# Strip 1's first product at two Strassen levels, with the further sums of W_in made by GpSimd in strip 0's second product and five of seven blocks used where they are made

## Chip, cores and metric

One core of one Trainium2 chip. The metric is the device time of one launch in microseconds (us). The engines are named PE (matrix products), DVE (VectorE), ACT (ScalarE), POOL (GpSimd) and SP, which here issues nearly all DMAs.

## The reference

```
kv  = einsum('bhsd,bhse->bhde', k, v)          # q, k, v: 8 x 8 x 576 x 64, f32
o   = einsum('bhsd,bhde->bhse', q, kv)
x   = o / sqrt(mean(o*o, -1) + 1e-6) * g_norm  # -> x: 4608 tokens x 512
h   = x @ w_in                                 # 512 x 2048
out = max(h, 0)**2 @ w_out                     # 2048 x 512
```

The attention part is small; the two products of the feed-forward part (x @ W_in, "first product", and g @ W_out, "second product", with g the squared relu) are nearly all of PE's work. w_in and w_out come as 64-bit floats, which the kernel turns into f32 itself.

## The kernel before

**Tiles and strips.** The 4608 tokens are nine strips of 512 (four tiles of 128). For each strip s the kernel does the first product, then the second. Meanwhile the queries of later strips are worked into x: a list of slices (`attend`, transposes, query products, means, roots, scaling, transposes of x), some after every step.

**Strassen.** The products are done with seven block products in place of eight (Winograd's form), on one or on two levels. Block sums of the weights are made once, those of x and g for each strip.

- Strip 0: first product plain (`up_first`); second product one level (`down`), in the order p = 1, 2, 5, 6, 7, 3, 4, two steps each: 14 steps, of which "step m" below is the m-th from 0. A block is 32 matmuls 128x256.
- Strip 1: first product one level (`up`: 4 groups g by 7 products p, 28 steps of 8 matmuls 128x256); second product two levels (`down_deep`).
- Strips 2 to 8: both on two levels: `up_slot` with 55 slots, in which 49 small products (`up_small`, 16 half-width matmul instructions each) run, then `down_deep`.

**The sums of the weights.** First-level sums of W_in: `sums_in(g)`, for each of four groups one scaling by g_norm on ACT (line 316) and four operations 128x512 on DVE (lines 318 and 306), at the steps 7, 8, 9 and 12 of strip 0's second product. The second-level ("deep") sums of W_out: `store_deep_sums(p, w)` after each block p of that product (4 operations 128x512 on DVE, `w_t` at line 306), stored to `w_deep` in DRAM by a DMA; strips 1 to 8 stream them back as `w_blk`. For p = 6 and p = 4 the four w_t are separate tiles of the `sum` pool with a store each (line 1000), for the others one tile of the `stream` pool with one store (line 1006). The second-level sums of W_in: `deep_sums_in(b)` for blocks b = 0 to 6, three POOL operations 128x512 each (lines 1219 and 306, tile `w_i`), made during strip 1's first product, stored to `w_in_deep` and streamed back by strips 2 to 8.

**What sets the order.** The order on each engine is the order in which the code writes it; nothing reorders. SP issues the DMAs in that same order, on one queue, with eight semaphores in turn, so a DMA is not issued before the eighth before it has landed. A pool hands out its tiles in turn: a new tile waits until all readers of its former contents, DMAs included, are done. `stream_pool` has 6 tiles of 1 MB, `sum_pool` 8 tiles of 256 KB, both opened where strip 0's second product starts. SP's queue around the change, in order: the stores of W_out's sums (`w_out<-wt`, `store_first` at line 344: 512 KB each), two loads `w_blk<-w_out` of 1 MB, two stores `w_deep<-w_t`, two of `store_first(2)`, a third `w_blk`, an output, k, v, k, v, a fourth `w_blk`, a `w_deep` store, the four stores of p = 6's w_t, the rest loads of k and v, queries.

**Names.** On PE the matmuls of a one-level product are line 870, those of two-level products line 865, the query products line 484 (`x_ps`), key-value products line 448 (`kv_ps`); ACT copies kv_ps to `kv_all` at lines 453 and 454, and query products read kv_all. Before block p = 3 of strip 0's second product, DVE makes `gq[21] - gq[11]` (line 306, 128x2048, `gt<-gt`; written at line 1034), which this block reads. `o_sb` at line 1042 is DVE's sum of a finished PSUM bank with a copy (`snap`) of another; it frees the bank for a later product. In strip 1's `up` the relu-square is DVE's lines 933 and 934.

Of the kernel before, what the change touches and what calls it, by code (L numbers as in the profile page):

```python
# [10 lines left out]
FP32 = mybir.dt.float32  # L11
# [9 lines left out]
def kernel(  # L21
# [52 lines left out]
    DEEP_UP = 2  # L74
# [3 lines left out]
    BEHIND = 1.6  # L78
    X_ON_PE = 2
# [234 lines left out]
    def sums_in(g):  # L314

        nc.scalar.activation(w_in[:, :, g, 0:4], w_in[:, :, g, 0:4], AF.Copy, scale=g_col)
        a11, a21, a12, a22, s1, s2, s4 = (block(b)[:, :, g] for b in range(7))
        nc.vector.tensor_tensor(out=s1, in0=a21, in1=a22, op=ALU.add)
        minus(nc.vector, s2, s1, a11)
        minus(nc.vector, s4, a12, s2)  # L320
        minus(nc.vector, a21, a11, a21)
# [366 lines left out]
    xc = {}  # L688

    def halves(s, kh, th):  # L690
        return xt[s][:, ts(th, TH // SQ), ts(kh, KH), :]

    def sums_x(s):
        xc[s] = t1, t2, t3, t4 = [
            sum_pool.tile([P, TH // SQ, KH, SQ], FP32, name=f"x_t{i}", tag="sum") for i in range(4)
        ]
        x = lambda kh, th: halves(s, kh, th)
        minus(nc.vector, t1, x(0, 1), x(0, 0))
        minus(nc.vector, t2, x(1, 1), t1)
        minus(nc.vector, t3, x(1, 1), x(0, 1))  # L700
        minus(nc.vector, t4, x(1, 0), t2)
# [218 lines left out]
    def up(s, g, p):  # L920
        open_bank(p)
        rhs = {
            1: halves(s, 0, 0), 2: halves(s, 1, 0), 3: halves(s, 1, 1),
            4: xc[s][3], 5: xc[s][0], 6: xc[s][1], 7: xc[s][2],
        }[p]
        for i in range(2):
            product(p, i, lambda kc: block(A_IN[p])[:, kc, g, ts(i, P)], lambda kc: rhs[:, :, kc, :], KH)
        dest = quarters(s, g)

        def relu_squared(q):  # L930
            def f(b, a):
                o = dest[q]
                nc.vector.tensor_tensor(out=o, in0=b, in1=a, op=ALU.add)
                nc.vector.scalar_tensor_tensor(out=o, in0=o, scalar=0.0, in1=o, op0=ALU.max, op1=ALU.mult)
            return f

        def last(b):
            nc.scalar.activation(dest[21], b, AF.Relu)
            nc.scalar.activation(dest[21], dest[21], AF.Square)

        combine(p, relu_squared(11), relu_squared(12), last, relu_squared(22))

# [3 lines left out]
    UP_SETS = (1, 6, 7, 5, 2, 3, 4)  # L946
    to_stream = [(s, p) for s in range(DEEP) for p in ORDER if (s, p) not in w_blk]
    for s in range(DEEP, N_STRIP):
        to_stream += [("in", s, p) for p in UP_SETS if s >= DEEP_UP]
        to_stream += [(s, p, n) for p in DEEP_ORDER for n in range(2)]  # L950
# [41 lines left out]
    def store_deep_sums(p, w):  # L992
        if p in (6, 4):

            parts = [sum_pool.tile([P, FQ // 2, P], FP32, name=f"w_t{i}", tag="sum") for i in range(4)]
            for _ in deep_sums(parts, w):
                if p == 4:
                    yield
            for i, t in enumerate(parts):
                nc.sync.dma_start(out=w_deep[B_OUT[p], :, i], in_=t)  # L1000
            return
# [3 lines left out]
        deque(deep_sums([t[:, i] for i in range(4)], w), 0)  # L1005
# [204 lines left out]

    def deep_sums_in(b):

        if b == 0:
# [289 lines left out]
```

## Time and profile before

| | |
|---|---|
| time, 3 runs | 868.7 us median (867.19 to 870.31) |
| profiled execution | 868.8 us, span of its instructions 867.0 us |
| granted TensorE clock | 1.000 |
| PE | 857.8 us busy, 99% |
| DVE | 702.0 us, 81% |
| ACT, POOL | 348.9 us (40%), 328.1 us (38%) |
| DMA | 236.46 MB, mean 273 GB/s |
| strip 0's second product | 83.1 to 138.25 us |
| strip 1's first product | 138.25 to 195.13 us |

How to read the rows of the prediction: a row of the timeline gives start, length (us), engine, line, operation, output tile <- input tiles, sizes and count, and in brackets the idle time before it with what ended it. A row of a table by stretches gives its limits and length, then the busy time of PE, PE's weight loads, DVE, ACT and POOL (number of instructions in brackets), the granted clock, the share of time in which the DMA engines were busy, and GB/s. A row of 40 digits gives the busy tenths of 40 equal slices of the span.

### The profile page before, as it was taken

Reading aid. Unit: us, or ns where it says so; the run is one execution under the profiler, and the core shown is the slowest. Engines: PE = TensorE matmul, PEld = TensorE weight load, DVE = VectorE, ACT = ScalarE, POOL = GpSimd, SP = SyncE. Lnnn points to the kernel's source line nnn. Section 1 sums busy time; section 2 is a strip of 40 time slices with the busy share of each in tenths; the row PEclk is TensorE's granted clock in tenths of the full one; section 3 lists DMA queues with packets and bytes.
Section 4 is the critical chain, followed back from the end, with each engine's and each line's share of the span. In section 5 each row is a group of like instructions: output and inputs, shape, how many; then the busy total and the mean of one; then the engine's idle time right before and its main releaser. Section 6 shows DMA issues by size and latency. Waiting matters only on the chain.

```text
span 867.0 us, 32426 instructions
## 1 busy us (share of the span) xinstructions
PE 857.8 (99%) x14176; PEld 804.2 (93%) x14176; DVE 702.0 (81%) x1132; ACT 348.9 (40%) x777; POOL 328.1 (38%) x335
## 2 busy tenths in 40 slices
PE   7999999999999999999999999999999999999998
PEld 6445888889999999999999999999999999999998
DVE  3768988879877996789688967897889777975887
ACT  4888241320048303750356034901491148102810
POOL 1223004630458223730574045704470447145700
PEclk9999999999999999999999999999999999999999
DMA  9898998999999997989698979987678856885583
GB/s 307 277 362 269 274 377 239 295 332 353 280 264 259 342 325 233 228 307 344 209 244 273 341 239 281 283 297 270 198 236 302 301 165 221 293 282 196 175 315 121
DMA packets 169469, 236.46 MB, mean 273 GB/s; under 512 B 78704, under 2 KB 133744, under 8 KB 161008
## 3 DMA queue, kind: packets, MB, share of 16 engines
q1 hardware_dynamic: 169024, 234.33, 83.5%
q8 instruction: 111, 1.82, 0.9%
q14 instruction: 30, 0.25, 0.1%
q10 hardware_dynamic: 304, 0.07, 0.0%
HBM read 197.66 MB, written 36.70 MB: 270 GB/s over the span
## 4 chain that ended last, share of the span: by engine, by line
PE 83%; DMA 7%; DVE 5%; ACT 3%; SPq 1%; issue 1%; DVEq 0%; ACTq 0%
PE ps_A L865 36%; PE ps_B L865 31%; PE ps_C L865 5%; PE ps_A L870 4%; DMA raw<-in_moe_w_in_dram 2%; PE kv_ps L448 2%; PE x_ps L484 2%; PE ps_B L870 2%; DVE w_t L306 1%; DMA w_deep<-w_t 1%; DMA raw<-in_moe_w_out_dram 1%; DMA w_blk<-w_deep 1%; PE ps_C L870 1%; DMA first_qkv<-in_v_dram 1%; ACT w_c L260 1%
## 5 line engine op out<-in xcount | busy, mean ns | idle before, releaser
L865 PE MATMUL ps_B<-w_blk,g_s 128*64 128x128 f32 x2016 | 122.0, 273 | 0.0
L865 PEld LDWEIGHTS ps_B<-w_blk,g_s 128*64 128x64 f32 x2016 | 112.6, 137 | 0.1
L306 POOL TENSOR_TENSOR x_l<-xT 128x256 f32<-128x256 f32 x21 | 16.2, 773 | 230.2 <-PE ps_A L865 230.2
L865 PE MATMUL ps_B<-w_blk,gt 128*64 128x128 f32 x1504 | 94.1, 273 | 0.3 <-DMA w_blk<-w_deep 0.3
L865 PE MATMUL ps_A<-w_blk,g_s 128*64 128x128 f32 x1536 | 92.2, 273 | 0.0
L1323 POOL TENSOR_TENSOR snap<-snap,gt 128x512 f32<-128x512 f32 x35 | 46.2, 1320 | 112.5 <-ACT snap L1328 93.6
L865 PEld LDWEIGHTS ps_A<-w_blk,g_s 128*64 128x64 f32 x1536 | 85.7, 137 | 0.0
L865 PEld LDWEIGHTS ps_B<-w_blk,gt 128*64 128x64 f32 x1504 | 84.6, 137 | 0.8 <-PE ps_B L865 0.5
L1328 ACT COPY snap<-ps_A 128x512 f32<-128x512 f32 x63 | 36.8, 585 | 103.6 <-PE ps_A L865 96.2
L1263 ACT ACTIVATE gt<-gt 128x512 f32<-128x512 f32 x112 | 70.2, 627 | 9.9 <-DVE gt L1323 9.9
L1264 ACT ACTIVATE gt<-gt 128x512 f32<-128x512 f32 x112 | 70.7, 631 | 3.5
L865 PE MATMUL ps_A<-w_blk,gt 128*64 128x128 f32 x1152 | 71.2, 273 | 0.0
L865 PEld LDWEIGHTS ps_A<-w_blk,gt 128*64 128x64 f32 x1152 | 64.7, 137 | 0.0
L1112 ACT COPY o_sb<-ps_A 128x128 f32<-128x128 f32 x24 | 6.4, 265 | 144.7 <-PE ps_A L865 109.4
L306 DVE TENSOR_TENSOR gt<-gt 128x2048 f32<-128x2048 f32 (+1 forms) x29 | 59.7, 2063 | 0.0
L1111 DVE TENSOR_TENSOR o_sb<-o_sb,ps_B 128x256 f32<-128x256 f32 (+1 forms) x123 | 47.4, 386 | 14.3 <-ACT o_sb L1112 9.5
L865 PE MATMUL ps_A<-x_l,w_in 128*64 128x128 f32 x896 | 58.6, 273 | 0.2 <-DVE gt L1323 0.2
L1323 POOL TENSOR_TENSOR gt<-gt,snap 128x512 f32<-128x512 f32 x42 | 52.5, 1279 | 15.1 <-DVE snap L1323 15.1
L865 PEld LDWEIGHTS ps_A<-x_l,w_in 128*64 128x64 f32 x896 | 50.8, 137 | 0.5 <-DVE gt L1323 0.5
L865 PE MATMUL ps_B<-x_l,w_blk 128*64 128x128 f32 x784 | 51.2, 273 | 0.0
L865 PE MATMUL ps_A<-x_l,w_blk 128*64 128x128 f32 x784 | 51.2, 273 | 0.0
L1112 ACT COPY o_sb<-ps_B 128x128 f32<-128x128 f32 x31 | 8.2, 265 | 96.3 <-PE ps_B L865 96.3
(214 smaller groups left out, 1900.2 us busy)
## 6 DMA issues: line engine op xcount, KB each, us to landing
w_blk<-w_deep SPq DMA_DIRECT2D x56, 1024.0 KB, 7.3
w_blk<-w_out SPq DMA_DIRECT2D x56, 768.0 KB, 6.2
w_blk<-w_in_deep SPq DMA_DIRECT2D x49, 768.0 KB, 5.8
raw<-in_moe_w_in_dram SPq DMA_DIRECT2D x16, 512.0 KB, 9.2
raw<-in_moe_w_out_dram SPq DMA_DIRECT2D x16, 512.0 KB, 8.0
k<-in_k_dram SPq DMA_DIRECT2D x29, 256.0 KB, 4.9
v<-in_v_dram SPq DMA_DIRECT2D x29, 256.0 KB, 5.2
x_d<-x_q SPq DMA_DIRECT2D x27, 256.0 KB, 4.8
```

Of the source, the lines that this page charges most:

```text
L260: nc.scalar.activation(c, high_f, AF.Copy, scale=EXPONENT)
L306: eng.tensor_tensor(out=out, in0=a, in1=b, op=ALU.subtract)
L448: nc.tensor.matmul(ps[ts(h, D), i], lhsT=a, rhs=w, start=i == 0 and c == 0, stop=c == C, skip_group_check=True)
L484: nc.tensor.matmul(ps[half, r, i, ts(p, D)], lhsT=q[row, half], rhs=kvd[b, p][row, row], start=True, stop=True)
L865: nc.tensor.matmul(ps[half], lhsT=lhsT[:, half], rhs=rhs, start=start, stop=stop, skip_group_check=True)
L870: nc.tensor.matmul(bank[BANK[p]][:, i, :], lhsT=lhsT(k), rhs=rhs(k), start=p in (1, 5, 2) and i == 0 and k == 0, stop=k == n - 1, skip_gro ...
L1111: add = lambda out, a, b: nc.vector.tensor_tensor(out=out, in0=a, in1=b, op=ALU.add)
L1112: yield nc.scalar.copy(q[:, 3:4], small(1))
L1263: nc.scalar.activation(o, o, AF.Relu)
L1264: nc.scalar.activation(o, o, AF.Square)
L1323: add = lambda eng, out, a, b: eng.tensor_tensor(out=out, in0=a, in1=b, op=ALU.add)
L1328: nc.scalar.copy(t, ps)
```

## The change

- Strip 1's first product becomes `up_slot`, on two levels; `up` and `sums_x` go. The sums of x for it (`leaf_x`, `sum_x`) are made by POOL, queued at step 8 of strip 0's second product.
- The scaling of W_in on ACT moves from steps 7, 8, 9, 12 to steps 0 and 1 (two instructions each); DVE's four operations of a pair of groups become 128x1024 and stand at steps 7 to 10, two a step.
- `deep_sums_in` moves into strip 0's second product: block 2 at step 1, block 3 at step 3, block 0 at 5, block 5 at 9, block 1 at 10; blocks 4 and 6 at the slots 2 and 24 of strip 1. Blocks 0, 2 and 3 are made in three tiles each of the `sum` pool and stored by three 256 KB DMAs, the others in a `stream` tile. The stores are queued on SP at the steps 3, 5, 7, 11 and 13 and at slots 8 and 31. Strip 1 reads blocks 0, 1, 4, 5 and 6 where they were made and streams 2 and 3 back.
- The w_t of p = 4, the last block, stay in SBUF for strip 1's second product (two loads fewer); they are made at the slots 38 to 43.
- `store_first` leaves out a quarter that nothing reads (256 KB of 1 MB, three times).
- In strip 1, the `snap` of j = 6 is DVE's sum instead of an ACT copy and a POOL sum. The pace of `attend` is halved per step, as there are twice as many.

The diff, cut to its core:

```diff
-    DEEP_UP = 2
+    DEEP_UP = 1
+    LATER = 2
...
+    SUMS_IN = {1: 2, 3: 3, 5: 0, 9: 5, 10: 1}
...
-    def sums_in(g):
-        nc.scalar.activation(w_in[:, :, g, 0:4], w_in[:, :, g, 0:4], AF.Copy, scale=g_col)
-        a11, a21, a12, a22, s1, s2, s4 = (block(b)[:, :, g] for b in range(7))
-        nc.vector.tensor_tensor(out=s1, in0=a21, in1=a22, op=ALU.add)
-        minus(nc.vector, s2, s1, a11)
-        minus(nc.vector, s4, a12, s2)
-        minus(nc.vector, a21, a11, a21)
+    def scales_in(h):
+        for g in range(2 * h, 2 * h + 2):
+            nc.scalar.activation(w_in[:, :, g, 0:4], w_in[:, :, g, 0:4], AF.Copy, scale=g_col)
+    def sums_in(h, n):
+        gs = slice(2 * h, 2 * h + 2)
+        a11, a21, a12, a22, s1, s2, s4 = (block(b)[:, :, gs] for b in range(7))
+        if n == 0:
+            nc.vector.tensor_tensor(out=s1, in0=a21, in1=a22, op=ALU.add)
+            minus(nc.vector, s2, s1, a11)
+        else:
+            minus(nc.vector, s4, a12, s2)
+            minus(nc.vector, a21, a11, a21)
...
     def store_first(b):
-        for e in range(2):
-            nc.sync.dma_start(out=w_out[b, :, e], in_=w_first[b][:, :, ts(e, P)])
+        for e, fs in enumerate((slice(FQ // 2, FQ), slice(0, FQ))):
+            nc.sync.dma_start(out=w_out[b, :, e, fs], in_=w_first[b][:, fs, ts(e, P)])
...
-    def up(s, g, p):
...
+    STORED_IN = (2, 3)
+        to_stream += [("in", s, p) for p in UP_SETS if s >= LATER or A_IN[p] in STORED_IN]
+        to_stream += [(s, p, n) for p in DEEP_ORDER for n in range(2) if s > DEEP or p != DEEP_ORDER[0]]
...
-                w_blk[u] = t.rearrange("p n f e -> p n (f e)")
-                nc.sync.dma_start(out=w_blk[u][:, 0:3], in_=w_in_deep[A_IN[p]].rearrange("p n g e -> p n (g e)"))
+                w = t.rearrange("p n f e -> p n (f e)")
+                nc.sync.dma_start(out=w[:, 0:3], in_=w_in_deep[A_IN[p]].rearrange("p n g e -> p n (g e)"))
+                w_blk[u] = [w[:, n] for n in range(3)]
...
     def store_deep_sums(p, w):
-        if p in (6, 4):
+        if p == 6:
...
-            for _ in deep_sums(parts, w):
-                if p == 4:
-                    yield
+            deque(deep_sums(parts, w), 0)
...
                 nc.sync.dma_start(out=w_deep[B_OUT[p], :, i], in_=t)
...
         t = deep.pop(p)
-        deque(deep_sums([t[:, i] for i in range(4)], w), 0)
+        if p == DEEP_ORDER[0]:
+            for j, x in zip((5, 6, 7, 4), range(4)):
+                w_blk[DEEP, p, j] = t[:, x]
+            for j, x in zip((3, 1, 2), ((0, 1), (1, 0), (1, 1))):
+                w_blk[DEEP, p, j] = w[:, x[0], ts(x[1], FQ // 2)]
+        for _ in deep_sums([t[:, i] for i in range(4)], w):
+            if p == DEEP_ORDER[0]:
+                yield
         nc.sync.dma_start(out=w_deep[B_OUT[p]], in_=t)
...
+    in_due = deque()
     def deep_sums_in(b):
...
-        if b == 0:
+        if b in (0, *STORED_IN):
...
+            t = [x.rearrange("p f e -> p (f e)") for x in t]
+            in_due.extend((w_in_deep[b, :, n].rearrange("p g e -> p (g e)"), x) for n, x in enumerate(t))
...
+            whole = whole[:, 0:3].rearrange("p n f e -> p n (f e)")
...
-        s1, s2, s4 = (x.rearrange("p f e -> p (f e)").rearrange("p (g e) -> p g e", g=2) for x in t)
+            in_due.append((w_in_deep[b].rearrange("p n g e -> p n (g e)"), whole))
+        s1, s2, s4 = (x.rearrange("p (g e) -> p g e", g=2) for x in t)
         nc.gpsimd.tensor_tensor(out=s1, in0=w_half(b, 0, 1), in1=w_half(b, 1, 1), op=ALU.add)
         minus(nc.gpsimd, s2, s1, w_half(b, 0, 0))
         minus(nc.gpsimd, s4, w_half(b, 1, 0), s2)
-        if b == 0:
-            for n, x in enumerate((s1, s2, s4)):
-                nc.sync.dma_start(out=w_in_deep[b, :, n], in_=x)
-            return
-        nc.sync.dma_start(
-            out=w_in_deep[b].rearrange("p n g e -> p n (g e)"), in_=whole[:, 0:3].rearrange("p n f e -> p n (f e)")
-        )
+        if b not in STORED_IN:
+            w_blk["in", DEEP_UP, next(p for p in UP_SETS if A_IN[p] == b)] = t
+    def store_sums_in():
+        while in_due:
+            to, x = in_due.popleft()
+            nc.sync.dma_start(out=to, in_=x)
...
         minus(nc.gpsimd, w_half(b, 0, 1), w_half(b, 0, 0), w_half(b, 0, 1))
...
+    MADE_IN, last_sums = {2: 4, 24: 6}, []
...
-        if slot in (1, 3, 5):
+        if slot in (1, 3, 5) and s > DEEP_UP:
...
-        if slot == 5:
+        if slot == 5 and s > DEEP_UP:
...
+        if s == DEEP_UP:
+            if slot in MADE_IN:
+                deep_sums_in(MADE_IN[slot])
+            if slot in (8, 31):
+                store_sums_in()
+            if slot == 38:
+                last_sums.append(store_deep_sums(*deep_due.popleft()))
+            if slot in (38, 39, 41, 43):
+                next(last_sums[0], None)
...
-                w = w_blk["in", s, p][:, (5, 6, 3).index(j), ts(i, P)]
+                w = w_blk["in", s, p][(5, 6, 3).index(j)][:, ts(i, P)]
...
-        if j == 3:
+        if j == 3 and (s > DEEP_UP or n in (1, 3, 5, 6)):
...
-            if j == 6 or before is None or p == 5:
+            if j == 6 and s > DEEP_UP or before is None or p == 5:
...
-        elif s == 0:
+        else:
...
-        else:
-            steps = [(1, up, (s, g, p)) for g in range(NG) for p in ORDER]
...
-        if s >= DEEP_UP:
-            goal = max(goal, min(ready[DEEP_UP] + (len(slices) - ready[DEEP_UP]) * (s - 1) // (N_STRIP - DEEP_UP - 1), len(slices)))
-            if s > DEEP_UP:
+        if s >= LATER:
+            goal = max(goal, min(ready[LATER] + (len(slices) - ready[LATER]) * (s - 1) // (N_STRIP - LATER - 1), len(slices)))
+            if s > LATER:
...
-                clock[0] += 3.2 if i >= n_up else 2.2 if s == DEEP else 1.2
+                clock[0] += 3.2 if i >= n_up else 1.1 if s == DEEP else 1.2
...
-                    attend(begun + (goal - begun) * min(i + 1, 25) // 25)
+                    attend(begun + (goal - begun) * min(i + 1, 50) // 50)
...
-                    attend_between(i, begun, goal, *(2, 34) if s == DEEP_UP else (0, 27), 38)
-                if s == DEEP and i in (3, 4, 7, 9):
-                    if i == 3:
-                        last_sums = store_deep_sums(*deep_due.popleft())
-                    next(last_sums, None)
-                if s == DEEP and i == n_up - 3:
-                    leaf_sums(s, 4)
-                if s == 1 and i in range(2, 23, 3):
-                    deep_sums_in((1, 6, 5, 4, 0, 2, 3)[i // 3])
-                if s == 1 and i in (17, 20, 21, 23):
-                    stream()
+                    attend_between(i, begun, goal, *(2, 34) if s == LATER else (0, 27), 38)
...
-            if i - n_up in (7, 8, 9, 12):
-                sums_in((7, 8, 9, 12).index(i - n_up))
-            if i == n_up + 11:
-                sums_x(1)
+            m = i - n_up
+            if m in (0, 1):
+                scales_in(m)
+            if 7 <= m < 11:
+                sums_in(*divmod(m - 7, 2))
...
-            pairs, m = divmod(max(n - 2 * NP, 0), 3)
-            attend(min(ready[0] + min(max(n, 0), 2 * NP) + (n >= 2 * NP) + 4 * pairs + (0, 2, 2)[m], goal))
+            pairs, third = divmod(max(n - 2 * NP, 0), 3)
+            attend(min(ready[0] + min(max(n, 0), 2 * NP) + (n >= 2 * NP) + 4 * pairs + (0, 2, 2)[third], goal))
             while deep_due and i not in (n_up + 1, n_up + 4, n_up + 12, n_up + 13):
                 deque(store_deep_sums(*deep_due.popleft()), 0)
+            if m in (3, 5, 7, 11, 13):
+                store_sums_in()
+            if m in SUMS_IN:
+                deep_sums_in(SUMS_IN[m])
+            if m == 8:
+                leaf_x(1, 0)
+                sum_x(1, 5)
+                sum_x(1, 6)
+                leaf_x(1, 1)
...
                 store_first(2)
```

More of the change, by code (lines that the diff above doesn't have):

```diff
@@ L686, in fetch_x @@
             )
-    xc = {}
     def halves(s, kh, th):
         return xt[s][:, ts(th, TH // SQ), ts(kh, KH), :]
[L693 to L701, printed above, removed]
     slices, ready = [], {}
@@ L918, in up_first @@
             nc.scalar.activation(dest[(11, 12, 21, 22)[2 * fh + th]][:, i, :], ps[:, ts(th, TH)], AF.Square)
-    def up(s, g, p):
[L921 to L941, printed above, removed]
     for p, t in zip((1, 2, 5), w_first):
@@ L946 @@
     UP_SETS = (1, 6, 7, 5, 2, 3, 4)
+    STORED_IN = (2, 3)
     to_stream = [(s, p) for s in range(DEEP) for p in ORDER if (s, p) not in w_blk]
     for s in range(DEEP, N_STRIP):
-        to_stream += [("in", s, p) for p in UP_SETS if s >= DEEP_UP]
-        to_stream += [(s, p, n) for p in DEEP_ORDER for n in range(2)]
+        to_stream += [("in", s, p) for p in UP_SETS if s >= LATER or A_IN[p] in STORED_IN]
+        to_stream += [(s, p, n) for p in DEEP_ORDER for n in range(2) if s > DEEP or p != DEEP_ORDER[0]]
     to_stream = iter(to_stream)
@@ L1360 @@
         attend(ready[s])
-        if s == DEEP_UP - 1:
+        if s == LATER - 1:
             while queried:
```

## The prediction

> **What bounds the kernel now.** I read the page's engine totals and chain, then the table by stages, then the single rows of the stages that the change touches.
>
> ```profile
> span 867.0 us, 32426 instructions
> PE   7999999999999999999999999999999999999998
> PE 83%; DMA 7%; DVE 5%; ACT 3%; SPq 1%; issue 1%; DVEq 0%; ACTq 0%
> ```
>
> PE is 99% busy (857.8 of 867.0 us): work taken off PE is time won, and a stall of PE anywhere is time lost, since no later slack takes it back. The question is whether the other engines keep up in the two stages that are rewritten: the second product of strip 0 (83 to 138 us) and the first of strip 1 (138 to 195 us).
>
> ```profile
> 83.00:138.25 55.25, 54.79 (x402) 47.59 (x397) 51.61 (x85) 16.71 (x26) 0.00 (x0) 1.00 0.98 321
> 138.25:195.13 56.88, 56.85 (x509) 48.79 (x508) 45.33 (x71) 16.62 (x34) 29.53 (x21) 1.00 0.94 289
> 232.80:290.00 57.20, 56.98 (x1162) 56.36 (x1160) 45.56 (x75) 34.12 (x84) 43.24 (x44) 1.00 0.97 271
> ```
>
> Columns: length, busy time of PE, its weight loads, DVE, ACT, POOL, then granted clock, DMA share, GB/s. The first row matters most: PE 54.8, DVE 51.6 and the DMA engines at 0.98, all in 55.25 us. Three resources are nearly full, and the change puts more DMAs and a new order on DVE there. POOL is idle, so its new work itself has room.
>
> **What the change gives.** One product of the strip at one level is 8 matmuls, and the next starts 1.73 us later; at two levels a small product is 16 half-size records, and the next starts 0.87 us later:
>
> ```profile
> 147.49 1.89 PE L870 MATMUL ps_A<-x_t,w_in 128*128 128x256 f32 x8
> 149.22 1.89 PE L870 MATMUL ps_B<-xT,w_s 128*128 128x256 f32 x8
> ```
>
> ```profile
> 236.23 1.04 PE L865 MATMUL ps_B<-w_blk,g_s 128*64 128x128 f32 x16
> 237.10 1.04 PE L865 MATMUL ps_C<-xT,w_in 128*64 128x128 f32 x16
> ```
>
> Strip 1's first product has 28 of the one (48.4 us) and gets 49 of the other (42.8 us): **-5.6 us**. PE's instructions change nowhere else.
>
> **What it costs in strip 0's second product.** The rows that decide:
>
> ```profile
> 116.73 7.14 PE L870 MATMUL ps_A<-w_blk,gt 128*128 128x256 f32 x32
> 123.71 7.07 PE L870 MATMUL ps_B<-w_blk,gt 128*128 128x256 f32 x32
> 131.24 7.17 PE L870 MATMUL ps_A<-w_blk,gt 128*128 128x256 f32 x32 [0.46 <-DVE o_sb L1042]
> 138.25 1.03 PE L870 MATMUL ps_A<-xT,w_in 128*128 128x256 f32 x4
> ```
>
> ```profile
> 115.39 0.69 DVE L306 TENSOR_TENSOR w_t<-w_s 128x512 f32<-128x512 f32 x1 [1.67 <-DMA w_deep<-w_t]
> 117.93 0.68 DVE L306 TENSOR_TENSOR w_t<-w_blk 128x512 f32<-128x512 f32 x1
> 119.26 0.68 DVE L306 TENSOR_TENSOR w_t<-w_blk 128x512 f32<-128x512 f32 x1
> 120.46 2.28 DVE L306 TENSOR_TENSOR gt<-gt 128x2048 f32<-128x2048 f32 x1
> 130.50 0.69 DVE L1042 TENSOR_TENSOR o_sb<-ps_A,snap 128x512 f32<-128x512 f32 x1
> ```
>
> (1) *The scales on ACT.* Two scalings of W_in (1.93 us each by their rows at 116 to 125 us) now stand in ACT's queue right ahead of the two kv_all copies that ran at 91.45 and 91.68. The copies end near 95.5 instead of 91.9, and PE's last query products, which read them, wait: a stall of 3.3 to 3.6 us at 92 us. By itself it would cost that; below it is covered by a longer wait. Where the scales stood before (116 to 125 us) they hid under ACT's idle time.
>
> (2) *The new wait of DVE.* The `sum` pool has 8 tiles. Before, the deep sums of W_out's block p=6 (the four w_t at 117.93 to 120.5) found it free. Now the W_in sums of blocks 2 and 3 take six of the tiles first, and the third and fourth w_t reuse tiles whose contents must first have been stored to `w_in_deep`. SP issues those stores late: behind block 2's three stores, the loads k, v, k, v, a W_out block (1 MB) and a w_deep store (1 MB). The transfers land in the order in which they are issued:
>
> ```profile
> w_deep<-w_t SPq DMA_DIRECT2D x4, 256.0 KB, 9.0
> ```
>
> That row (median from issue to landing) belongs to the transfers that came at this point of the queue before; they were issued from 122.45 and landed from 131.53 to 133.48, 0.6 to 0.7 us apart, and the 1 MB ahead of them at 130.93. So the queue, not the issue, sets the time. In the changed kernel the first stores of W_out are cut by 3 x 256 KB (their 512 KB took 1.9 to 2.7 us each, so about 3.2 us less) and block 2 adds 3 x 256 KB (2.0 us): the 1 MB lands near 129.8, the two stores that free the tiles at 130.4 and 131.1. I allow 129.5 to 133.5 for the second, because the stall of (1) may let the queue run dry. Behind the two waiting w_t in DVE's order stands the `gt` difference (2.28 us) that PE's block p=3 reads. It ends at 131.1 + 0.7 + 2.3 = 134.1, and PE starts that block at about 134.2 instead of 123.71: **+10.5 us** (+8.8 to +12.8), 3.5 of it the stall of (1), 7 us a second one. Before, the same difference ended at 122.7, one us early: that us was all the cover there was.
>
> (3) *What DVE still has to do after it.* Before, DVE used its 9 us of sums between 122.7 and 131.8 beside the block; the last but one block's start was already late by 0.46 us, for `o_sb`. Now each of the two remaining blocks (7.1 us of PE) has 8.0 us of DVE beside it: four halves of sums_in of 1.2 us, four or so w_t (2.5 us) and `o_sb` (0.7 us). PE needs that `o_sb`, since it frees the PSUM bank. That is +1 us for each of two blocks. On top comes POOL, now at work beside DVE:
>
> ```profile
> 142.07 0.68 DVE L933 TENSOR_TENSOR gt<-ps_C,snap 128x512 f32<-128x512 f32 x1
> 142.79 1.42 DVE L934 SCALAR_TENSOR_TENSOR gt<-gt 128x512 f32<-128x512 f32 x1
> ```
>
> While POOL ran (from 142.4 us), DVE's operations on SBUF alone took up to 1.42 us where they take 0.69 else; those that read PSUM kept 0.68. With x sums and W_in sums on POOL at 131 to 150 us this costs 0 to 2.5 us per block. I take +1.3 for each. So strip 1 starts 10.5 + 2 x (1 + 1.3) = about **+15 us** later (near 153; +12 to +18). The four `x_t` of DVE (2.5 us) that went to POOL stood behind the last `o_sb` and give nothing here.
>
> **What it costs in strip 1.** POOL now starts strip 1 with six W_in sums of 1.3 to 1.7 us, a difference and two x operations, about 14 us, the first of them behind DVE's last w_t; PE wants the result 12.5 us after its start: 1 to 1.5 us. DVE gets five snaps more (0.67 us each) and has about 53 us of work in a stage that shrinks from 56.9 to 51 us: 0 to 4 us. The query loads, whose transposition kept DVE waiting 2.91 us at 161.8 before, have less time after the stores but also a later start: 0 to 1 us. Together 0 to 6.6, of which I take **+2.5**, nearer the POOL row than the DVE end, as DVE in the third stage row does the same kind of work with 45.6 of 57.2 us. The two loads saved for the deep block kept in SBUF lie on the DMA queue alone: nothing, hidden by PE.
>
> **Sum.** 15 - 5.6 + 2.5 = +11.9 us on the profiled execution, 868.8 us (span 867.0 and 1.8 around it), which stands 0.1 above the median of 868.7: 880.7, forecast **881 us**; with the bounds of the parts 875 to 886.
>
> **The rivals.**
> (a) *The stores are no wait*: PE keeps its order and the gain shows. For that the two stores would have to land by 124 us, 7 us sooner than the queue gives (p=3 wants its operand 3.6 us after 123.7, and 3.6 us of DVE lie between). Then 868.8 - 5.6 + 0 to 2.5 = 863 to 866, faster, say **865**. For it: PE's own saving is certain. Against it: DMA share 0.98 and 9 us from issue to landing. Chance 0.14. If in that case the stall of (1) stays alone, 868.8 + 3.5 - 5.6 + 2.5 = **869**, no change: 0.06.
> (b) *DVE becomes the bound in both stages*: every bound at its upper end, +18 - 5.6 + 6.6 = +19, **888 us**. For it: DVE 51.6 of 55.25 us; against: the third stage row. Chance 0.10.
> (c) *The long stalls slow PE's clock.* In this trace the clock is 1.00 in every stretch, and no wait of PE is longer than 1.4 us, so it shows nothing on stalls of 7 us. If the clock were halved for one to two blocks of 1.7 us after each of two stalls, the first would be covered and the second add 1.7 to 3.4 us: **883 to 884**, chance 0.10. The Trainium skill, "TensorE: Matmul & The Clock Gate", Part 1, states such a rule: after an idle window of about 3.4 us the array runs at half clock until it has been busy about as long. By it the sum would be about 1.7 us higher; no run here shows it yet.
> The forecast without (c) holds 0.60.
>
> **How the numbers follow.** Faster by over 0.3% (2.6 us, about what a measurement of this kernel can tell from no change) is (a): 0.14. Within it: 0.06. Slower: 0.60 + 0.10 + 0.10 = 0.80. The range reaches down to the edge of (a), 866, and up over (b), 889; what lies outside is most of (a) and a little above (b).
>
> **What would show it.** In the new trace: PE idle 3.5 us at 92 us, ended by ACT's kv_all copy; DVE idle some 8 to 11 us before a w_t of block p=6, ended by a DMA `w_in_deep<-w_i`; PE's block p=3 at about 134 us; strip 1 at about 153; its 49 small products 0.87 us apart with small gaps. If DVE's wait at 120 us is missing, or strip 1 starts before 145, the forecast is wrong by its main term. If strip 1's stage takes over 57 us, (b) holds.

## The result, and the profile after

The changed kernel takes 903.0 us (median of 4 runs, 899.6 to 907.8) against 868.0 for the kernel before (4 runs): ratio 1.0405, 95% interval 1.0348 to 1.0463. It is slower by about 35 us; the forecast was 881, with 889 as the upper end. The profiled execution is the fastest of the four (899.6 us), so its trace accounts for 30.8 of the 35 us.

From its page: the span, PE's busy tenths, the granted clock, and the chain.

```profile
span 897.8 us, 33638 instructions
PE   8999867888999999999999999999999999999998
PEclk9999998899999999999999999999999999999999
PE 82%; DVE 6%; DMA 4%; POOL 3%; issue 3%; ACT 2%; SPq 1%; DVEq 0%; POOLq 0%
```

A slice is 22.4 us. PE's holes are slices 5 to 10 (digits 8, 6, 7, 8, 8, 8; about 90 to 224 us), strip 0's second product and strip 1's first; in slices 7 and 8 (135 to 180 us) the mean clock is below 90%, which it was in no slice before. POOL is in the chain for the first time. PE's busy time rose by 4.5 us (857.8 to 862.3) though its matmuls ask for 5.6 us less, so 10.1 us came on top. Its idle time rose by 26.3 us (9.2 to 35.5). -5.6 + 10.1 + 26.3 = +30.8, the difference of the spans (867.0, 897.8). Of the 10.1 us, 8.0 are the clock: PE worked 16.0 us at a granted clock of 0.50, in four stretches (the clock is the number behind POOL's). What the other 2 us are stays open.

```profile
93.98:97.39 3.41, 3.41 (x21) 2.70 (x15) 2.34 (x4) 1.09 (x2) 3.25 (x3) 0.50 0.59 175
134.26:138.35 4.09, 4.09 (x10) 3.28 (x11) 4.02 (x3) 0.00 (x0) 3.93 (x4) 0.50 0.96 279
157.15:162.25 5.10, 5.10 (x68) 4.65 (x70) 0.69 (x1) 0.82 (x2) 4.94 (x5) 0.50 0.94 302
216.86:220.27 3.41, 3.41 (x36) 3.41 (x34) 3.27 (x9) 1.16 (x3) 1.26 (x1) 0.50 0.70 252
```

What PE waited for (total, times, longest):

```profile
PE ps_B L865 <- DVE gt L308: 7.0, 1, 7.0
PE ps_A L860 <- DVE snap L1318: 4.2, 2, 2.9
PE ps_A L860 <- DVE o_sb L1021: 3.9, 1, 3.9
PE ps_A L860 <- DVE gt L1318: 3.4, 1, 3.4
PE x_ps L491 <- ACT kv_all L460: 3.0, 1, 3.0
PE ps_B L860 <- DVE snap L1318: 2.9, 1, 2.9
PE ps_A L865 <- DVE o_sb L1021: 2.6, 1, 2.6
```

The rows that answer to those at 116 to 138 us before (lines have moved: 870 is now 865 for strip 0, the two-level products are 860, DVE's 306 is 308):

```profile
134.26 9.18 PE L865 MATMUL ps_B<-w_blk,gt 128*128 128x256 f32 x32 [7.02 <-DVE gt L308]
146.05 7.17 PE L865 MATMUL ps_A<-w_blk,gt 128*128 128x256 f32 x32 [2.61 <-DVE o_sb L1021]
157.15 1.98 PE L860 MATMUL ps_A<-xT,w_in 128*64 128x128 f32 x16 [3.92 <-DVE o_sb L1021]
```

```profile
130.65 0.69 DVE L308 TENSOR_TENSOR w_t<-w_blk 128x512 f32<-128x512 f32 x1 [8.14 <-DMA w_in_deep<-w_i]
131.31 0.69 DVE L308 TENSOR_TENSOR w_t<-w_blk,w_t 128x512 f32<-128x512 f32 x1
131.92 2.28 DVE L308 TENSOR_TENSOR gt<-gt 128x2048 f32<-128x2048 f32 x1
134.12 1.75 DVE L324 TENSOR_TENSOR w_s<-w_in 128x1024 f32<-128x1024 f32 x1
...
145.32 0.68 DVE L1021 TENSOR_TENSOR o_sb<-ps_A,snap 128x512 f32<-128x512 f32 x1
```

The wait for the stores that free the tiles is there to the microsecond (PE's block p=3 at 134.26, forecast 134.2). New to the reader are two things: that block takes 9.18 us where it took 7.07, though PE waits for nothing in it (the clock), and DVE's first operation on 128x1024 takes 1.75 us where 1.2 was reckoned (POOL). By stages (columns as before; the second row ends at PE's stall before the 44th of the 49 small products):

```profile
81.50:157.15 75.65, 59.12 (x397) 50.07 (x397) 62.06 (x78) 17.22 (x27) 32.05 (x21) 0.92 0.75 256
157.15:216.00 58.85, 48.59 (x972) 46.32 (x972) 38.34 (x66) 19.20 (x39) 39.02 (x40) 0.96 0.73 205
```

DMA share fell from 0.98 to 0.75 in the first: the queue that was full now stands still at times. SP's rows show why:

```profile
122.48 9.87 SPq L972 DMA_DIRECT2D w_deep<-w_t  x4
...
135.47 2.47 SPq L128 DMA_DIRECT2D q<-in_q_dram  x4
145.42 0.34 SPq L985 DMA_DIRECT2D w_deep<-w_t  x1
146.02 0.41 SPq L957 DMA_DIRECT2D out_dram<-o_sb  x1
156.43 0.33 SPq L985 DMA_DIRECT2D w_deep<-w_t  x1
157.03 0.39 SPq L957 DMA_DIRECT2D out_dram<-o_sb  x1
157.47 1.24 SPq L128 DMA_DIRECT2D q<-in_q_dram  x1
```

Between 138 and 157.4 us SP issues two stores and two outputs, each behind a late DVE, and the next queries stand behind them until strip 1 has begun. In strip 1 DVE then waits for queries, and PE for DVE (the 2.9 and 3.4 us above):

```profile
DVE qT L407 <- DMA q<-in_q_dram: 9.0, 2, 4.7
```

Strip 1's two products, from its first matmul to strip 2's, took 97.1 us before (138.25 to 235.35) and take 107.9 now (157.15 to 265.02), where 91.5 would be the old time less the 5.6.

### The profile page after: what moved, and what is told of

Read it like the earlier page. It is cut to its first block, busy times and chain, and to the rows that moved or that the text cites. A ratio compares the mean times of both kernels' runs of the same rounds, so it can differ in the third digit from the quotient of the medians.

```text
span 897.8 us, 33638 instructions
## 1 busy us (share of the span) xinstructions
PE 862.3 (96%) x14736; PEld 811.9 (90%) x14736; DVE 711.7 (79%) x1138; ACT 360.7 (40%) x796; POOL 364.8 (41%) x370
## 4 chain that ended last, share of the span: by engine, by line
PE 82%; DVE 6%; DMA 4%; POOL 3%; issue 3%; ACT 2%; SPq 1%; DVEq 0%; POOLq 0%
PE ps_A L860 35%; PE ps_B L860 31%; PE ps_C L860 5%; PE ps_A L906 2%; DVE w_t L308 2%; PE kv_ps L455 2%; PE x_ps L491 2%; PE ps_C L906 2%; PE ps_B L906 1%; DMA k<-in_k_dram 1%; DMA w_deep<-w_t 1%; DMA first_qkv<-in_v_dram 1%; PE ps_A L642 1%; PE ps_A L865 1%; POOL w_i L308 1%
## 5 line engine op out<-in xcount | busy, mean ns | idle before, releaser
L308 POOL TENSOR_TENSOR x_l<-xT 128x256 f32<-128x256 f32 x24 | 20.8, 865 | 223.9 <-PE ps_A L860 213.2
L1248 ACT ACTIVATE gt<-gt 128x512 f32<-128x512 f32 x128 | 80.2, 626 | 19.0 <-DVE gt L1318 15.8
L860 PEld LDWEIGHTS ps_B<-w_blk,gt 128*64 128x64 f32 x1488 | 86.6, 137 | 0.3 <-issue 0.3
L1323 ACT COPY snap<-ps_A 128x512 f32<-128x512 f32 x67 | 39.3, 586 | 111.3 <-PE ps_A L860 103.3
L1249 ACT ACTIVATE gt<-gt 128x512 f32<-128x512 f32 x128 | 80.8, 631 | 4.1
L1318 POOL TENSOR_TENSOR gt<-gt,snap 128x512 f32<-128x512 f32 x48 | 60.1, 1281 | 34.0 <-DVE snap L1318 33.8
L860 PE MATMUL ps_A<-x_l,w_in 128*64 128x128 f32 x1024 | 68.8, 273 | 2.3 <-DVE snap L1318 1.3
L860 PEld LDWEIGHTS ps_A<-x_l,w_in 128*64 128x64 f32 x1024 | 59.8, 137 | 2.8 <-issue 1.5
L860 PE MATMUL ps_A<-x_l,w_blk 128*64 128x128 f32 x816 | 54.9, 273 | 2.9 <-DVE snap L1318 2.9
L860 PE MATMUL ps_B<-x_l,w_blk 128*64 128x128 f32 x816 | 56.0, 275 | 0.5 <-issue 0.5
L860 PE MATMUL ps_A<-x_l,w_s 128*64 128x128 f32 x768 | 52.6, 276 | 4.0 <-DVE gt L1318 3.4
```

The costliest lines, as they stand in the source:

```text
L308: eng.tensor_tensor(out=out, in0=a, in1=b, op=ALU.subtract)
L860: nc.tensor.matmul(ps[half], lhsT=lhsT[:, half], rhs=rhs, start=start, stop=stop, skip_group_check=True)
L1248: nc.scalar.activation(o, o, AF.Relu)
L1249: nc.scalar.activation(o, o, AF.Square)
L1318: add = lambda eng, out, a, b: eng.tensor_tensor(out=out, in0=a, in1=b, op=ALU.add)
L1323: nc.scalar.copy(t, ps)
```

## Experiments

Below, "strip 1 from" is its first matmul and "takes" the time to strip 2's first, both in the profiled execution; the ratios to the kernel before are those of each run's own chip. Line numbers shift by one where an edit adds a line.

| run | median us | strip 1 from | takes |
|---|---|---|---|
| before | 868.0 | 138.25 | 97.1 |
| changed | 903.0 | 157.15 | 107.9 |
| e1_block3_later | 900.3 | 150.57 | 113.2 |
| e2_scales_later | 900.4 | 147.08 | 115.0 |
| e3_queries_early | 897.6 | 158.67 | 103.1 |
| e4_before_delayed | 881.7 | 149.33 | 97.7 |
| e5_queries_and_order | 902.9 | 145.24 | 118.8 |
| e6_faster_drips | 903.1 | 147.11 | 119.8 |
| e7_deep_sums_earlier | 905.9 | 158.72 | 109.7 |
| e8_sums_in_later | 898.0 | 140.93 | 120.0 |
| f1_wait_removed | 894.8 | 149.56 | 110.8 |
| f2_wait_scales_queries | 892.2 | 149.68 | 103.9 |
| f3_block6_earlier | 888.6 | 147.99 | 101.8 |
| f4_x_sums_later | 884.5 | 143.98 | 105.4 |
| g1_both_pool_moves | 883.1 | 143.39 | 103.7 |
| g2_output_sums_first | 884.7 | 139.19 | 109.8 |
| g3_deep_sums_at_30 | 887.2 | 138.66 | 114.9 |
| g4_differences_first | 890.5 | 138.27 | 115.9 |
| g5_sums_tighter | 887.6 | 139.16 | 110.4 |

Most medians are of two runs; single runs of one kernel lay up to 8 us apart (the changed kernel's), and the runs come from several chips, on which the kernel before took 868.0 to 870.6 us. So differences under 4 us are not decided by the medians, and I read the traces for them.

**e1: the wait for tiles, removed by moving POOL's work.**

```diff
-    SUMS_IN = {1: 2, 3: 3, 5: 0, 9: 5, 10: 1}
+    SUMS_IN = {1: 2, 9: 0, 10: 5, 11: 1}
-    STORED_IN = (2, 3)
+    STORED_IN = (2,)
-    MADE_IN, last_sums = {2: 4, 24: 6}, []
+    MADE_IN, last_sums = {2: 4, 24: 6, 30: 3}, []
-        if j == 3 and (s > DEEP_UP or n in (1, 3, 5, 6)):
+        if j == 3 and (s > DEEP_UP or n in (1, 5, 6)):
```

> The changed kernel, but W_in's block 3 is made in strip 1 (slot 30, in a stream tile, used where made, stored after), and block 0 at step 9, blocks 5 and 1 at steps 10 and 11, so that the w_t of p=6 find free tiles. Both theories: DVE's 8.1 us wait for the stores is gone, p=3 starts 7 to 10 us earlier, at about 125 to 127 us with the clock at 1.00, strip 1 near 143 to 147. Theory A (the wait also causes strip 1's excess, since SP stood at the late w_t stores and the queries came late): strip 1's two products take about 94 us in place of 107.9, the time is 866 to 874 us. Theory B (strip 1 is short of DMA and DVE time by itself): they still take 103 to 108 us, the time is 884 to 892 us.

900.3 us: both theories fell. The wait went as both said, and p=3 runs at 127.73 without a stall, but strip 1 starts at 150.57, later than the 143 to 147 that both gave, and takes 5 us more than in the changed kernel. PE's rows:

```profile
127.73 7.07 PE L865 MATMUL ps_B<-w_blk,gt 128*128 128x256 f32 x32
138.99 8.67 PE L865 MATMUL ps_A<-w_blk,gt 128*128 128x256 f32 x32 [4.19 <-DVE o_sb L1021]
150.57 1.09 PE L860 MATMUL ps_A<-xT,w_in 128*64 128x128 f32 x16 [2.91 <-DVE o_sb L1021]
```

POOL's x sums, which had waited for the same tiles, now run beside DVE's sums, and these take from 123.3 (the difference) to 138.9 (o_sb). In strip 1 DVE waits 12.2 us for queries and PE 5.5 us for POOL, which has block 3 as well. The saving was handed on, not kept.

**e2: the scales behind the kv_all copies**, on top of e1 (`scales_in(1)` after `attend` at step 1).

> As e1_block3_later, and the second pair of ACT's scalings is queued after the kv_all copies of step 1. If the 3.0 us stall of PE at 92 us is ACT's, it goes here, and without a longer wait behind it the time falls by 2 to 3 us against e1_block3_later; if DVE's sums are the bound of the stage anyway (theory of DVE as the bound), it falls by under 1 us.

The stall of 3.0 us at 92 us is gone and strip 1 starts 3.5 us earlier (147.08), but takes 1.8 more. The median is the same, 900.4, of two executions 6 us apart (897.4 and 903.4). The profiled one is the slower: it reaches strip 2 1.7 us before e1 and loses 5 us after that, where PE waits for a load of W_out's sums, which e1's trace doesn't have:

```profile
317.45 1.97 PE L860 MATMUL ps_B<-w_blk,gt 128*64 128x128 f32 x16 [3.80 <-DMA w_blk<-w_deep]
```

So half of that stall's price was paid again in strip 1; whether the rest is won, two executions don't decide.

**e3: the queries early**, in the changed kernel.

```diff
-            if i in (n_up + 8, n_up + 11):
-                load(2, (i - n_up) // 11, nc.sync, "q")
-            if i == n_up + 12:
+            if i == n_up + 8:
+                for p in range(2):
+                    load(2, p, nc.sync, "q")
                 load_q_rest(2, nc.sync)
```

> The changed kernel, but the loads of batch 2's second queries and its rest are issued with the first ones at step 8, ahead of the late stores of w_t and the outputs. Nothing of strip 0's stalls changes (strip 1 starts at 155 to 158 us). Theory A: the waits of DVE for queries in strip 1 (4.3 and 4.7 us) and the PE stalls behind them (2.9 and 3.4 us) fall to under 3 us together, the time falls by 4 to 8 us, to 892 to 898. Theory B: they stay, the time within 3 us of the changed kernel's 899 to 908.

897.6 us; strip 1 starts at 158.67, a little after the 155 to 158 expected, and takes 103.1 instead of 107.9. DVE's wait for queries falls from 9.0 to 4.8 us, and PE's stalls behind it from 6.3 to 2.2. SP's queue order was worth some 5 us, as theory A had it for this part.

**e4: one stall by itself**, in the kernel before.

```diff
         if p == (2 if s else 6):
+            for _ in range(4):
+                dly = small.tile([P, 1], FP32, name="dly", tag="dly")
+                nc.vector.reduce_sum(out=dly, in_=gq[s, 22].rearrange("p f t -> p (f t)"), axis=AX.X)
             minus(nc.vector, gq[s, 21], gq[s, 21], gq[s, 11])
```

> The kernel before with four needless sums over 128x2048 on DVE (about 2.2 us each, 8.8 in all, results unused) ahead of the difference that block p=3 reads. It measures the price of one stall of PE by itself. If a long stall slows PE's clock: PE idle 7 to 8 us before p=3, that block at 9 us instead of 7.1 with a granted clock near 0.8, and 11 to 14 us in all (880 to 883). If not: block 7.1 us, clock 1.00, 8 to 10 us (877 to 879).

881.7 us, 12.1 above the kernel before on its chip (ratio 1.0151, 1.0096 to 1.0205), as expected if a stall slows the clock. The row and the stretch around it:

```profile
133.03 9.56 PE L870 MATMUL ps_B<-w_blk,gt 128*128 128x256 f32 x32 [8.44 <-DVE gt L306]
```

```profile
117.00:145.00 28.00, 19.56 (x82) 16.54 (x81) 27.66 (x32) 8.91 (x7) 0.00 (x0) 0.82 0.83 287
```

PE idles 8.4 us, and the 32 matmuls behind it take 2.5 us more with nothing to wait for. POOL is idle here and the program else the same, so it is the idle time that slows the clock. Strip 1 itself (97.7) is untouched.

**e5 to e8: more of strip 1's work earlier or later.** e5 is e2 with e3's edit and block 3 at slot 18; e6 adds a query load in every slot (`least = 1.0`); e7 is the changed kernel with the w_t of p=4 at slots 14 to 20; e8 is e6 with `sums_in` at steps 9 to 12 and POOL's blocks 5 and 1 at steps 12 and 13.

> e2_scales_later with batch 2's queries loaded early (the edit of e3_queries_early) and block 3's sums at slot 18 in place of 30. Strip 0 as in e2_scales_later: strip 1 starts at 146 to 149 us. Theory Q (in strip 1 DVE waits for query loads that come too late, and this is most of the stage's excess): the waits fall from 12 to under 6 us, both products of strip 1 take under 106 us, time 886 to 892. Theory J (the jam of DVE and POOL at slots 35 to 45 decides the end of the stage whenever the queries come): strip 2 starts at 260 to 262 us whatever is early, time 896 to 900.

> As e5_queries_and_order, and in strip 1 a query load is issued in every slot, not in every second one. Theory Q: DVE waits for queries under 2 us in strip 1, another 3 to 6 us less than e5_queries_and_order (880 to 888). Theory J: no more than 1 us.

> The changed kernel, but the four w_t of p=4 are made at slots 14, 16, 18 and 20 of strip 1 (where DVE stands waiting for queries) and not at 38 to 43. Theory J: the PE stalls at 213 and 222 us (2.9 and 1.3 us, ended by DVE's snap) go, with the slow clock after the first, 4 to 6 us in all (894 to 899 by the fastest run). Theory Q: they shrink by under 1 us, since DVE is late there with work of the queries.

> As e6_faster_drips, but DVE's first-level sums of W_in stand at steps 9 to 12 in place of 7 to 10, with blocks 5 and 1 of POOL behind them at steps 12 and 13. If PE's stalls for o_sb in strip 0 (5.3 and 2.3 us in e2_scales_later) come from the work that stands ahead of o_sb in DVE's queue, stretched by POOL, they fall to under 2 us together and strip 1 starts 4 to 7 us earlier, at 141 to 143 us; what is left goes to strip 1, where POOL's sums for block 5 come later by as much: if PE waits for them there, the time falls by under 2 us.

902.9, 903.1, 905.9 and 898.0 us: only e8 gained, 5 us on the changed kernel. Theory Q fell for e5 and e6: one wait for queries of 7.8 to 7.9 us stayed, and PE's waits for POOL grew to 9.9 us (6.3 at `w_s`, 3.6 at `w_in`), since block 3 now stood in POOL's queue ahead of what PE needed (the longest of them moved from 209 us in e2 to 188 in e5, as block 3 had moved from slot 30 to 18). In e7 the stall of 2.9 us at 213 went, as theory J had it, and a wait for POOL of 3.6 us took its place. In e8 strip 1 starts at 140.93, within 3 us of before, as expected (one stall of 2.5 us for o_sb is left), and then waits 15.2 us for POOL; the time falls by 5.1 us against e6 all the same, where under 2 was expected. In e5, e7 and e8 what one wait lost, another engine's wait took back, wholly or for the most part.

**f1 to f4: the wait removed without giving POOL more work.** f1:

```diff
-            parts = [sum_pool.tile(...) for i in range(4)]
+            parts = [sum_pool.tile(...) for i in range(2)]
+            parts += [w[:, 0, ts(0, FQ // 2)], w[:, 1, ts(1, FQ // 2)]]
...
-            while deep_due and i not in (n_up + 1, n_up + 4, n_up + 12, n_up + 13):
+            while deep_due and i not in (n_up + 1, n_up + 4, n_up + 6, n_up + 12, n_up + 13):
```

> The changed kernel, but the deep sums of p=6 come after the difference that block p=3 reads, and two of the four are written over the W_out block they are made from, so that they need no tiles of blocks 2 and 3; POOL's work stays as in the changed kernel. DVE's 8.1 us wait and PE's 7.0 us stall go; strip 1 starts at 145 to 150 us in place of 157. Theory W (the wait alone makes strip 1 late, its own excess stays): strip 1's products take 106 to 110 us, the time falls by 7 to 12 us. Theory P (strip 1's end is pinned by what does not move with its start, the query loads above all): they take 113 us or more, the time falls by under 4 us.

f2 adds e2's and e3's edits, f3 moves POOL's block 6 to slot 12 in f2, f4 moves `if m == 8` of the x sums to `if m == 12` in f2.

> f1_wait_removed with the second pair of scalings behind the kv_all copies and batch 2's queries loaded early. No PE stall at 92 us; theory P: DVE waits for queries of 8 us or more fall to under 5, strip 1's products to 100 to 104 us, the time 880 to 890 us. If both the wait for tiles and the queries are beside the point, it stays over 895.

> f2_wait_scales_queries with POOL's sums of block 6 at slot 12 in place of 24. If POOL's chain (sums, then the difference that PE reads) is what holds PE at the middle of strip 1, PE's waits for POOL fall from a few us to under 1 us and the time by 2 to 5 us; if POOL only follows DVE there, the time stays within 1.5 us.

> f2_wait_scales_queries with POOL's x sums queued at step 12 in place of 8, so that POOL stands idle beside DVE's chain of sums. If POOL stretches DVE's operations on SBUF, DVE's work from the difference to the second o_sb (16.0 us of operations where nothing shares the time) falls towards 16 to 18 us and PE's stalls for o_sb to under 2 us together; strip 1 then waits for the x sums instead: 2 to 5 us at its slots 4 to 8. If DVE is long by itself, it stays over 20 us.

f1: 894.8, 8.2 less than the changed kernel; strip 1 starts 7.6 us earlier and takes 2.9 more: theory W, though 110.8 lies over its edge of 110. DVE's waits for queries stay, 9.3 us. f2: 892.2; the waits for queries fall to 3.5 us and strip 1 takes 103.9, but PE still stalls 2.7 and 6.3 us for o_sb, which the expected 880 to 890 left out. f3: 888.6, the size expected but not for the reason: PE's waits for POOL were 0.9 us already in f2, and what shrank were waits for DVE (snap 4.2 to 1.5, o_sb 6.3 to 4.8). The second can't be the edit's, since f3 is the same program up to slot 12 of strip 1; without it about 2 us of the 3.6 are left. f4: 884.5, 7.7 less than f2. My figure of 16 us for DVE's work left out the four w_t of p=6 that f1 had put behind the difference; with them it is about 21, so the 20 us at which DVE was to be called long by itself was the wrong mark. PE's two stalls for o_sb fell from 8.9 to 5.5 us, not to under 2. From the difference to the end of the second o_sb DVE takes 28.1 us in f2 (121.44 to 149.53) and 24.7 in f4 (119.13 to 143.83). The stretches, f2 and then f4:

```profile
122.00:150.00 28.00, 19.09 (x90) 16.22 (x90) 27.32 (x23) 0.58 (x1) 18.96 (x13) 0.97 0.85 288
```

```profile
119.10:144.00 24.90, 19.37 (x91) 16.43 (x89) 24.52 (x24) 0.58 (x1) 9.52 (x5) 0.99 0.88 294
```

DVE is busy throughout in both with the same operations; POOL is at 19.0 us in the one and 9.5 in the other. Half of POOL's work beside it is gone, and with it 3.4 of the 7 us by which DVE was above its 21.

**g1 to g5: is strip 1's excess order or amount?** g1 is f3 and f4 together. g2 puts DVE's w_t of p=7 and p=3 behind the o_sb of their steps, the second half of `sums_in` at steps 11 and 12, blocks 5 and 1 at 12 and 13, the x sums at 11. g3 is g2 with the w_t of p=4 at slots 30 to 35. g4 and g5 are g2 with blocks 5, 1, 4, 6 at slots 0, 4, 9, 16 and 0, 3, 8, 12.

> f4_x_sums_later with POOL's sums of block 6 at slot 12 (the edit of f3_block6_earlier). If the two moves act on separate waits, the gains add: 12.. us under f2_wait_scales_queries less 7.7 and 3.6, so 880 to 882 us. If they act on one chain, 884 to 886.

> g1_both_pool_moves with DVE's work put behind what PE waits for: the w_t of p=7 and p=3 after the o_sb of their step, the second half of sums_in at steps 11 and 12, POOL's blocks 5 and 1 at 12 and 13 and the x sums at 11. If PE's stalls for o_sb at the end of strip 0 (1.6 and 3.9 us) are DVE's queue order, they go, and strip 1 starts at 139 to 141 us; the time falls by 4 to 6 us unless strip 1 then waits for POOL by as much.

> g2_output_sums_first with the four w_t of p=4 at slots 30 to 35 in place of 38 to 43. If DVE's jam at slots 38 to 45 is what remains of strip 1's excess, PE's stalls of 3.0 and 1.3 us there shrink by half or more, and the time falls by 2 to 4 us; if the jam only moves, under 1 us.

> g2_output_sums_first, but POOL's sums for blocks 5, 1, 4 and 6 are made at the slots 0, 4, 9 and 16 of strip 1, so that the difference of block 0, for which PE waited 7.7 us, is first in POOL's queue. If the order is what is left, this wait falls under 1 us and no other takes its place: 873 to 878 us. If POOL's amount is the bound in the first half of strip 1 (it worked without a break from 131 to 173 us in g2), the wait comes back at the sums of block 5 or 1: 880 to 885 us.

> As g4_differences_first with blocks 1, 4 and 6 at slots 3, 8 and 12. If POOL's amount is the bound, within 2 us of g4_differences_first; if its order within the slots is, 2 to 4 us apart.

g1 is the best version, 883.1 us, ratio 1.0154 (1.0100 to 1.0207): still slower than before, so none of these can be recommended. The moves of f3 and f4 add only in part, between the two outcomes expected. g2 removes every stall for o_sb, as expected (strip 1 from 139.19, where before had 138.25), and PE waits at once for POOL:

```profile
PE ps_A L860 <- POOL w_in L308: 7.7, 1, 7.7
```

g3 doesn't gain: PE's waits for DVE's snaps are 4.7 us (1.6 in g2), so the jam, that is, more work for DVE in a few slots than they last, only moved. g4 and g5 bring the 7.7 us at `w_in` down to 0.7, and waits for POOL at `x_t` (3.6) and `w_s` (1.1 and 2.0) take its place. But g4's 890.5 us lie above both outcomes expected, and POOL is not all of it: DVE waits 11.9 us for queries in g4 and 12.9 in g5 (4.0 in g2), and in g4 the wait for a tile that a store of W_in's sums must free is back, with 5.3 us of PE behind it:

```profile
196.64 0.69 DVE L308 TENSOR_TENSOR w_t<-w_blk 128x512 f32<-128x512 f32 x1 [6.64 <-DMA w_in_deep<-w_i]
```

POOL's load, in g1's first 39 us of strip 1:

```profile
143.15:182.00 38.85, 35.57 (x664) 33.72 (x666) 24.59 (x44) 8.80 (x19) 34.80 (x39) 0.91 0.72 221
```

POOL is busy 34.8 of 38.85 us (90%), where before strip 2, which POOL serves alike but for the W_in sums and the snaps of j=6, has 43.2 of 57.2 (76%). So in the first half of strip 1 the amount of POOL's work is close to the time. That it is the bound there is argued, not shown: PE waits for POOL only 2.5 us in g1, the longest stall of its strip 1 (2.6 us, ending at 195.6) is put down to no engine, and no run took work off POOL. g4 and g5 differ by 2.9 us with intervals that overlap (1.0188 to 1.0267, 1.0151 to 1.0221), so order within the slots isn't told apart. Not tried: these sums on an engine other than POOL.

## Why the prediction was wrong

*Its main mechanism was right, to the microsecond.* DVE waited 8.14 us for `w_in_deep<-w_i` (8 to 11 said), PE 7.02 (7 said), block p=3 started at 134.26 (134.2), PE stalled 2.97 us at 92 us, ended by ACT's copy (3.3 to 3.6). f1 shows that the wait was worth about 8 us of the result. (The four transfers of before that I timed the wait by stand 0.2 us later in the trace than I wrote, issued from 122.68; nothing hangs on it.)

*The term of what DVE does after it was too small.* I took 9.3 us for each of the two remaining blocks; DVE took 11.8 and 11.1 (from 134.12 to 145.92 and to 157.00). POOL's contention was 3 to 4 us each, not 1.3: I priced it on operations 128x512 (0.69 to 1.42) and capped it at 2.5; here operations 128x1024 went from 1.22 to 2.28 and w_t from 0.69 to 1.75. f4 against f2 shows it as POOL's. That POOL stood idle in this stage gave its new work room, as I said, but DVE paid for it. Strip 1 began 18.9 us late in place of 15.

*The step that failed is "What it costs in strip 1 ... I take +2.5", with 0 to 6.6 as its bounds.* The stage and its second product lost 10.8 us where -3.1 was forecast: 16.4 us of costs against 2.5. That is 13.9 of the 18.9 us by which the profiled execution (+30.8) missed the sum of +11.9; strip 0 makes 3.9 and the strips after it 1.1. I priced each engine's amount of work and each wait by itself. What came: DVE's waits for queries (9.0 us, with 6.3 of PE behind them), since SP's queue is in order and part of the loads stood behind stores that wait for the late DVE (loading them ahead of the stores took 4.2 of the 9.0 away, e3; removing the wait for tiles alone took nothing away, f1); the jam of DVE at slots 38 to 45 (4.2 us of PE); POOL, 1.0 us at first, to which the wait moves when others are removed (e5 to e8, g2 to g5); and the clock, 4.3 us (the last two of the four stretches at 0.50). Together 15.8 of the 16.4. I listed the queries as "0 to 1 us" because the stage starts later; I forgot that the loads are issued by the same queue that waits.

*Rival (c) was no rival but part of the outcome.* I gave the slow clock a chance of 0.10 and a cost of 1.7 to 3.4 us, for two stalls. It came after four of the stalls and took 8.0 us of PE's time: 3.8 in strip 0, which DVE's lateness covered, since PE stood waiting for DVE again behind both of those stretches, and 4.3 in strip 1, which counted. So the two stalls that I had found cost nothing by their clock; I left out those that would follow.

*The gain is there, but no version shows it as time won:* where nothing holds them up, the 49 small products stand 0.87 us apart (164.97, 165.85, 166.72 us ...), as the 5.6 us were reckoned. How to have it without the costs stays open; no version run here has shown it.

## What to carry to other kernels

Where PE is 99% busy and, in the stage that changes, DVE is at 93% and the DMA engines are at 98%, take a stall that is found and priced as a lower bound: here in-order queues handed it on (DVE late, so SP late, so queries late, so DVE late), and PE paid again. Price a move by what stands behind it in every queue, the DMA issuer's above all, and price a stall of PE at its length plus what the clock takes after it, here up to 1.7 us for each slow window of 3.4 us (see below), unless another wait covers that. And when an edit removes a stall and the time doesn't move, look for the queue that took it over: e1, e2, e5, e6 and e8 moved strip 1's start by 7 to 16 us and gained 0 to 5.

## What the runs showed of the hardware

*The clock after idle time.* Stalls of PE of 3.9 us and more were each followed by slow matmuls: 3.92 us (first small products 1.98 and 1.95 us in place of 1.04), 4.19 (e1: block 8.67 in place of 7.1), 7.02 (9.18), 8.44 (e4: 9.56). After shorter ones it varied: 2.97 and 2.94 us were followed by slow work (16 matmuls in 5.24 us instead of 3.62; the rows below), 2.61, 2.90 and 3.38 were not, but one of 2.46 us in e8 was (two small products 1.27 and 1.92 us long from start to start).

```profile
212.05 1.09 PE L860 MATMUL ps_B<-xT,w_i 128*64 128x128 f32 x16
216.08 1.28 PE L860 MATMUL ps_A<-x_l,w_blk 128*64 128x128 f32 x16 [2.94 <-DVE snap L1318]
217.15 1.92 PE L860 MATMUL ps_A<-x_l,w_s 128*64 128x128 f32 x16
```

The Trainium skill, "TensorE: Matmul & The Clock Gate", Part 1, puts this down to an activity window of about 3.4 us that runs on its own, not from the start of the stall. The changed kernel's trace agrees as to the half speed (granted clock 0.50 from 157.15 to 162.00 us, behind the stall of 3.92) and as to the window: the clock goes to 0.50 at 93.98, 131.53, 155.42 and 216.86 us, which are 11, 7 and 18 times 3.413 us apart, and stays there for 3.41, 6.83, 6.83 and 3.41 us. In each of the other traces the stretches also begin on one such grid and last one, two or three of its windows.

What decides is how long PE idles within one window of this grid, not how long the stall is. The stall of 3.92 us puts 2.2 us into one window, and the next is slow; that of 3.38 us falls half into one window and half into the next (2.0 and 1.4 us), and neither is followed by a slow one. PE's busy time is the second number of a row, the clock the third from the end:

```profile
152.01:155.42 3.41, 1.21 (x6) 0.73 (x4) 3.38 (x3) 0.59 (x1) 2.56 (x2) 1.00 0.00 0
155.42:158.83 3.41, 1.68 (x16) 1.71 (x18) 1.58 (x3) 0.00 (x0) 2.22 (x2) 0.50 0.47 192
179.31:182.73 3.42, 1.44 (x44) 1.30 (x40) 0.00 (x0) 0.52 (x2) 0.00 (x0) 1.00 0.81 171
182.73:186.14 3.41, 2.01 (x37) 1.84 (x41) 3.25 (x6) 0.00 (x0) 0.00 (x0) 1.00 0.75 111
```

Counted over the 18 traces of all runs but the kernel before, from 60 to 350 us: after a window at full clock in which PE idled over 1.98 us the next was slow, 58 times of 58; with under 1.89 us never, 1392 times; between the two, 3 times of 6. After a slow window the next was fast when PE idled under 0.46 us in it (54 of 54) and slow with 0.77 us or more (30 of 30). So in this kernel a stall of 2 to 4 us costs a slow window or not by where it falls on the grid, which the program doesn't set: the same stall of 2.97 us at 92 us was followed by slow work in the changed kernel, e7 and f1, and not in e1 and e3.

*POOL beside DVE slows both.* POOL's x_l on 128x256, 0.72 us alone, took 2.85 us at 131.94 in the changed kernel while DVE's difference ran; DVE's 128x1024 took 2.28 us in place of 1.22. The same pair of engines a little later, with POOL idle and then at work:

```profile
147.16 1.22 DVE L308 TENSOR_TENSOR w_s<-w_s,w_in 128x1024 f32<-128x1024 f32 x1
148.87 1.90 POOL L1204 TENSOR_TENSOR w_i<-w_s 128x512 f32<-128x512 f32 x1 [4.03 <-issue]
149.56 2.29 DVE L308 TENSOR_TENSOR w_in<-w_in 128x1024 f32<-128x1024 f32 x1
```

In all the traces together, DVE's 48 operations on 128x1024 beside an idle POOL took 1.21 to 1.23 us, the 88 others 1.22 to 2.30. DVE's sums of 128x512 that read PSUM took at most 0.70 us in either case. Work on POOL that looks free in an idle POOL is paid by DVE when DVE is the engine that PE waits for.
